# First LayerNorm shared between VectorE and ScalarE, with a new load order, five staging buffers and a split K load, in a fused attention and gated-GLU kernel

## Chip, cores and metric

The kernel runs on one core of one Trainium2 chip. The metric is device time in microseconds (us) for one launch. Eight runs of the kernel before took between 320.76 and 323.88 us, with a median of 322.65 us.

## What is computed

The input is 2048 rows (the sequence) by 640 features, in bf16. A LayerNorm without weights is followed by two branches that read the same normalized rows: causal attention with a sliding window of 256 keys in 32 heads of 20 features, and a gated unit with 1536 hidden features. The output is the sum of the input and both branches.

```python
xn = layernorm(A_x)                              # over 640 features, eps 1e-5
q, k, v = split(xn @ wqkv)                       # 32 heads of 20
p = softmax(mask(q @ k.T * 20 ** -0.5))          # 0 <= i - j < 256
attention = (p @ v) @ wo
h = sigmoid(xn @ w_gate) * (xn @ w_up)           # 2048 x 1536
out = A_x + attention + h @ w_down
```

## The kernel before

**Tiling.** The 2048 rows are handled as four chunks of 512 (`c`), each of four blocks of 128 rows (`s`). A chunk is normalized (`xn`, rows on the partitions) and transposed into `xnT` (features on the partitions). Chunk 0 is transposed by TensorE with an identity matrix and a copy out of PSUM (`transpose_block`, L266); chunks 1 to 3 by a transposing DMA (`turn_block`, L273).

**Projections.** `proj_block` (L283) makes 128 features of q or k for a whole chunk: five matmuls of 128x512 into one PSUM tile, a copy to a bf16 staging tile `st` (VectorE for q, ScalarE for k), and a DMA that stores it to a DRAM scratch (`sq`, `sk`). `spread` (L300) loads the scratch back as `qT` or `kT`, with each head at its own partitions. Ten such projections make a chunk: five for q, then five for k. Staging tiles rotate through the pool `stp` of four buffers; the first of them is first used as the zero operand of the warm-up matmuls. V is projected per block in two halves of 320 columns (`proj_v`, L313) and copied to `v`.

**Order of the work.** Every engine runs its instructions in the order in which the program issues them; there is no scheduler. The program has these stages.

- Start: loads are issued, mostly on SyncE's queue (SP): the four blocks of chunk 0 (two of them on ScalarE's queue), the V columns of `wqkv` in two pieces, its q and k columns, the first halves of the gate and up weights, chunk 1, and two DMAs (`clear`, L186) that write zeros into the scratch. Eleven matmuls on zeros keep TensorE busy in the meantime.
- First LayerNorm (L564 to L583): two blocks at a time. VectorE takes the statistics of a block in two halves and aggregates them (L243, L248), ScalarE takes the square root (L554), VectorE the reciprocal and the normalization (L558, L262), TensorE transposes, and ScalarE copies to `xnT` (L271). V projections are put between the steps of blocks 2 and 3, with copies on ScalarE.
- q and k of chunk 0 (`g_qk(0)`, L585), back to back.
- The main loop (L629). Each step issues the score matmuls, exponentials and masks of some heads, and then pulls as much other TensorE work from a list, `fill`, as a running credit allows. The list (L597 to L615) is in a fixed order: gate and up of chunk 0, q, k and V of chunk 1, two gate and up blocks of chunk 1, output of chunk 0, q and k of chunk 2, and so on. The LayerNorm of a later chunk is a generator (`g_norms`, L326) that `mix` (L543) draws from: one draw after every so many pieces of the host generator. For chunk 2 the hosts are `gu1a` (every second piece) and `out0` (every third piece).
- The end: the last output products with all of PSUM.

**Around the change in the main loop.** The `kT` load of chunks 1 to 3 is issued inside `g_v` (L362), after V of the first block; the four DMAs that rearrange the output weights `wo` in DRAM (`turn_wo`, L212) and the four that load them (`load_wo`, L217) stand behind it on SP's queue. The output rows `y` are staged in the pool `yp` of two buffers for chunks 0 to 2, and in the `xn` tiles (four buffers) for chunk 3.

PSUM tiles: one in `ps_a` (tile `acc`), three that rotate for all projections, gate, up and output (`ps_d`), and one of four times that size for scores.

Of the kernel before, what the change touches and what calls it, by code (L numbers as in the profile page):

```python
# [9 lines left out]
P = 128  # L10
S = 2048
D = 640
H = 32
DH = 20
F = 1536
DC = D // P
FC = F // P
CW = 512
NCH = S // CW
SBC = CW // P  # L20
HG = 4
NG = H // HG
GH = NG // 2
VW = DH + 1
# [5 lines left out]
ADD = mybir.AluOpType.add  # L30
MULT = mybir.AluOpType.mult
# [3 lines left out]
BF16 = mybir.dt.bfloat16  # L35
FP32 = mybir.dt.float32
EXP = mybir.ActivationFunctionType.Exp
TANH = mybir.ActivationFunctionType.Tanh
SQRT = mybir.ActivationFunctionType.Sqrt

U = 64
PTW = 10 * U
# [67 lines left out]
def kernel(  # L110
# [11 lines left out]
    nc = tc.nc  # L122
# [4 lines left out]
    def pool(name, bufs, **kw):  # L127
        return ctx.enter_context(tc.tile_pool(name=name, bufs=bufs, **kw))
# [2 lines left out]
    xp = pool("xp", 3)  # L131
    lnp = pool("lnp", 4)
    xtp = pool("xtp", 2)
    stp = pool("stp", 4)
    qp = pool("qp", 2)
    kp = pool("kp", 3)
    vp = pool("vp", 10)
# [3 lines left out]
    onp = pool("onp", 2)  # L141
    tp = pool("tp", 1)
    np_ = pool("np", 1)
    yp = pool("yp", 2)
    ps_a = pool("ps_a", 1, space=bass.MemoryType.PSUM)
    ps_d = pool("ps_d", 3, space=bass.MemoryType.PSUM)
    banks = ctx.enter_context(ExitStack())
# [5 lines left out]
    xc = {}  # L153
# [15 lines left out]
    def load_wqkv(part):  # L169
        nc.sync.dma_start(out=wqkv[:, :, part * D:(part + 1) * D],  # L170
                          in_=wqkv_r[:, :, part * D:(part + 1) * D])

    xc[0] = xp.tile([P, SBC, D], BF16, name="xc")
    for s, queue in ((0, nc.sync), (1, nc.scalar), (2, nc.sync), (3, nc.scalar)):
        queue.dma_start(out=xc[0][:, s, :], in_=xr[:, s, :])
    for d in (slice(0, 3), slice(3, DC)):
        nc.sync.dma_start(out=wqkv[:, d, 2 * D:], in_=wqkv_r[:, d, 2 * D:])
    load_wqkv(0)
    load_wqkv(1)

# [46 lines left out]
    eps = const.tile([P, 1], FP32, name="eps")  # L227
    nc.gpsimd.memset(eps, EPS)
    scr = const.tile([P, 1], FP32, name="scr")
    nc.scalar.activation(out=scr, in_=eps, func=SQRT)  # L230
    for n in (6, 5):
        ps = ps_d.tile([P, CW], FP32, name="pwarm", tag="d")
        for k in range(n):
            nc.tensor.matmul(ps, lhsT=warm[:, 0:P], rhs=warm, start=(k == 0), stop=(k == n - 1))


    xnT = {}
    xns = {}

    def ln_half(c, s, a, stats=None):  # L240
        if a == 0:
            stats = lnp.tile([P, 2, nc.vector.BN_STATS_DIM], FP32, name="stats")
        nc.vector.bn_stats(out=stats[:, a, :], in_=xc[c][:, s, a * HALF:(a + 1) * HALF])  # L243
        return stats

    def ln_mv(stats):
        mv = lnp.tile([P, nc.vector.BN_AGGR_DIM], FP32, name="mv")
        nc.vector.bn_aggr(out=mv, in_=stats)  # L248
        return mv

    def ln_block(c, s):
        return ln_mv(ln_half(c, s, 1, ln_half(c, s, 0)))
# [5 lines left out]
        return rstd  # L258

    def norm_block(c, s, mv, rstd):  # L260
        xn = lnp.tile([P, D], BF16, name="xn", bufs=4)
        nc.vector.tensor_scalar(out=xn, in0=xc[c][:, s, :], scalar1=mv[:, 0:1],  # L262
                                scalar2=rstd[:, 0:1], op0=SUB, op1=MULT)
        xns[c, s] = xn

    def transpose_block(c, s):  # L266
        xn = xns.pop((c, s))
        pt = ps_d.tile([P, DC, P], BF16, name="pt", tag="d")
        for d in range(DC):
            nc.tensor.transpose(pt[:, d, :], xn[:, d * P:(d + 1) * P], ident)  # L270
        nc.scalar.copy(out=xnT[c][:, :, s * P:(s + 1) * P], in_=pt)  # L271

    def turn_block(c, s):  # L273
        nc.sync.dma_start(out=xnT[c][:, :, s * P:(s + 1) * P], in_=xns.pop((c, s)), transpose=True)
# [1 line left out]
    def new_xnT(c):  # L276
        xnT[c] = xtp.tile([P, DC, CW], BF16, name="xnT")
# [3 lines left out]
    vt = {}  # L281
# [18 lines left out]
    def spread(w, c, g0, g1):  # L300

        if g0 == 0:
            qk[w, c] = (qp if w == "q" else kp).tile([P, NG, CW], BF16, name=w + "T")
        src = scratch[w, c % 2].rearrange("(g p) s -> p g s", p=P)
        nc.sync.dma_start(out=qk[w, c][:, g0:g1, :], in_=src[:, g0:g1, :])

    def new_v(c, s):
        v = vp.tile([P, H * VW + 11], BF16, name="v")
        vt[c * SBC + s] = v
        nc.gpsimd.memset(v[:, 0:H * VW].rearrange("p (h d) -> p h d", d=VW)[:, :, DH:VW], 0.5)  # L310
        nc.gpsimd.memset(v[:, H * VW:], 0.0)

    def proj_v(c, s, hf):  # L313
        v3 = vt[c * SBC + s][:, 0:H * VW].rearrange("p (h d) -> p h d", d=VW)
        ps = ps_d.tile([P, CW], FP32, name="pv", tag="d")
        for d in range(DC):
            nc.tensor.matmul(ps[:, 0:HALF], lhsT=xnT[c][:, d, s * P:(s + 1) * P],  # L317
                             rhs=wqkv[:, d, 2 * D + hf * HALF:2 * D + (hf + 1) * HALF],
                             start=(d == 0), stop=(d == DC - 1))
        copy = nc.vector.tensor_copy if c else nc.scalar.copy  # L320
        copy(out=v3[:, hf * 16:(hf + 1) * 16, 0:DH],  # L321
             in_=ps[:, 0:HALF].rearrange("p (h d) -> p h d", d=DH))

    MM = 216

# [36 lines left out]
    def g_v(c):  # L362
        for s in range(SBC):
            new_v(c, s)
            for hf in range(2):
                proj_v(c, s, hf)
            if s == 0:
                spread("k", c, 0, NG)
            yield 10 * 136


# [36 lines left out]

    def outp(c, s, ys, last=False):
        sb = c * SBC + s  # L410
        if c == NCH - 1:
            y = lnp.tile([P, D], BF16, name="xn", bufs=4)
        else:
            y = yp.tile([P, D], BF16, name="y_sb")

        def wo_half(hf):
            for m in range(DC):
                nc.tensor.matmul(ys[hf], lhsT=oc[c, m][:, s * P:(s + 1) * P],  # L418
                                 rhs=wo[:, m, hf * HALF:(hf + 1) * HALF],
                                 start=False, stop=(m == DC - 1))  # L420

        def add_half(hf):
            nc.vector.scalar_tensor_tensor(  # L423
                out=y[:, hf * HALF:(hf + 1) * HALF], in0=ys[hf], scalar=0.5,
                in1=xc[c][:, s, hf * HALF:(hf + 1) * HALF], op0=MULT, op1=ADD)

        if last:
            for hf in range(2):
                wo_half(hf)
                add_half(hf)  # L430
                cut = slice(hf * HALF, (hf + 1) * HALF)
                (nc.scalar, nc.sync)[hf].dma_start(out=out2[sb * P:(sb + 1) * P, cut], in_=y[:, cut])
        else:
            wo_half(0)
            wo_half(1)
            add_half(0)
            add_half(1)
            nc.sync.dma_start(out=out2[sb * P:(sb + 1) * P, :], in_=y)
        yield 10 * 136

    def g_out(c):
        for s in range(SBC):
            ys = [ps_d.tile([P, CW], FP32, name=f"y{i}", tag="d")[:, 0:HALF] for i in range(2)]
            yield from down(c, s, ys)
            yield from outp(c, s, ys)
# [97 lines left out]
    def mix(a, b, first, every=1, rest=True):  # L543

        for k, cost in enumerate(a):
            yield cost
            if k >= first and (k - first) % every == 0:
                yield next(b, 0)
        if rest:
            yield from b  # L550

    def root(mv):
        r = lnp.tile([P, 1], FP32, name="rstd")
        nc.scalar.activation(out=r, in_=mv[:, 1:2], func=SQRT, bias=eps)  # L554
        return r

    def norm_turn(s, mv, r):
        nc.vector.reciprocal(r, r)  # L558
        norm_block(0, s, mv, r)

    new_xnT(0)
    for s in range(SBC):
        new_v(0, s)
    for s in (0, 2):  # L564
        mv0 = ln_block(0, s)
        r0 = root(mv0)
        if s:
            proj_v(0, 0, 0)
            proj_v(0, 0, 1)
        half = ln_half(0, s + 1, 0)  # L570
        norm_turn(s, mv0, r0)
        mv1 = ln_mv(ln_half(0, s + 1, 1, half))
        r1 = root(mv1)
        if s:
            proj_v(0, 1, 0)
        transpose_block(0, s)
        norm_turn(s + 1, mv1, r1)
        if s:
            proj_v(0, 1, 1)
        transpose_block(0, s + 1)  # L580
    for s in (2, 3):
        for hf in range(2):
            proj_v(0, s, hf)  # L583
    nc.scalar.activation(out=scr, in_=neghalf, func=EXP)
    for _ in g_qk(0):  # L585
        pass
# [2 lines left out]
    fill = Fill()  # L589
    GU = 10 * MM  # L590
    OUT = 4 * 34 * 136
    def later(load, *args):
        load(*args)
        yield 0

    norms2 = g_norms(2, True)
# [5 lines left out]
    fill.add("wo_i", later(turn_wo), 0)  # L602
    fill.add("gu1a", mix(g_gu(1, 0, 2), norms2, 0, 2, False), 2 * GU)
    fill.add("wo", later(load_wo), 0)
    fill.add("out0", mix(g_out(0), norms2, 0, 3), OUT)
    fill.add("x3", later(load_x, 3), 0)
    fill.add("qk2", g_qk(2), 50 * MM)
    fill.add("v2", g_v(2), 40 * 136)
# [37 lines left out]
    c = NCH - 1  # L646
# [15 lines left out]
    for s in range(SBC):  # L662
        run(outp(c, s, ys[s], s == SBC - 1))
# [28 lines left out]
```

## Time and profile before

The profiled execution took 326.08 us, of which the span from the first to the last instruction is 324.0 us; its mean granted TensorE clock is 0.995.

| engine | busy us | share of the span | instructions |
|---|---|---|---|
| TensorE matmuls (PE) | 310.6 | 96% | 4391 |
| TensorE weight loads (PEld) | 174.6 | 54% | 4391 |
| ScalarE (ACT) | 192.4 | 59% | 240 |
| GpSimd (POOL) | 177.6 | 55% | 417 |
| VectorE (DVE) | 159.6 | 49% | 325 |

Some rows of the first 16 us, from the groups by line and shape:

| line, engine | what | count | mean ns |
|---|---|---|---|
| L243 DVE | statistics of half a block, 128x320 | 8 | 473 |
| L248 DVE | aggregate | 4 | 209 |
| L554 ACT | square root, 128x1 | 4 | 295 |
| L558 DVE | reciprocal, 128x1 | 4 | 164 |
| L262 DVE | normalize, 128x640 bf16 | 4 | 446 |
| L271 ACT | copy of a transposed block out of PSUM, 128x640 bf16 | 4 | 687 |
| L321 ACT | copy of half a V block out of PSUM, 128x320 | 8 | 426 |

Times are from the start of the span. In a list in order of time, each row has its start, its length, the engine, the line, the operation, what it writes and reads, the shape and a count; in brackets is how long the engine was idle before, and what ended that wait. SPq is SyncE's queue of DMA issues: its times are those of issuing a DMA, not of its transfer. Transfers land later. PEclk is the granted TensorE clock as a share of the full one.

### The profile page before, as it was taken

The numbers are of one execution on the slowest core, as the hardware profiler recorded it, in microseconds if no ns is written. First come the engines' busy times: TensorE is split into PE (matmuls) and PEld (weight loads), VectorE is DVE, ScalarE is ACT, GpSimd is POOL, SyncE is SP. The second block draws the span as 40 slices with busy tenths as digits, with TensorE's granted clock in tenths as the row PEclk, the third lists the DMA queues.
The fourth block names the chain that finished last, engine by engine and source line by source line (L and its number), as shares of the span: only waits on it lengthen the run. The fifth ranks groups of instructions, "written<-read, shape, count | busy, mean of one in ns | idle before, by whom it ended". The sixth has DMA issues, their size and how long they took to land.

```text
span 324.0 us, 10258 instructions
## 1 busy us (share of the span) xinstructions
PE 310.6 (96%) x4391; PEld 174.6 (54%) x4391; DVE 159.6 (49%) x325; ACT 192.4 (59%) x240; POOL 177.6 (55%) x417
## 2 busy tenths in 40 slices
PE   6979999999899979999999999999999999999996
PEld 2634444455466645644466655544456664444674
DVE  5330287574864433745954352754352444463224
ACT  3803586878564447766665457566766568778200
POOL 3000269567586827475793647556474857586400
PEclk9997999999999999999999999999999999999999
DMA  7964786946641452540035123710000000000002
GB/s 247 375 250 129 262 297 76 292 151 197 206 128 42 92 146 85 181 131 3 2 22 89 36 71 91 243 45 3 2 2 22 23 26 21 2 2 2 0 2 81
DMA packets 34380, 33.05 MB, mean 102 GB/s; under 512 B 9600, under 2 KB 33792, under 8 KB 34304
## 3 DMA queue, kind: packets, MB, share of 16 engines
q1 hardware_dynamic: 33904, 32.01, 33.2%
q8 instruction: 34, 0.56, 0.7%
q10 hardware_dynamic: 432, 0.41, 0.4%
q14 instruction: 10, 0.08, 0.1%
HBM read 21.00 MB, written 10.26 MB: 96 GB/s over the span
## 4 chain that ended last, share of the span: by engine, by line
PE 78%; DMA 9%; DVE 6%; ACT 2%; POOL 2%; issue 1%; SPq 1%; DVEq 0%; ACTq 0%; POOLq 0%
PE pg L382 14%; PE pu L389 13%; PE y L402 13%; PE pqk L290 12%; PE ps L455 7%; PE acc L486 6%; PE y L418 6%; PE pv L317 4%; DMA sq<-st 2%; DMA wo_i<-in_A_wo_dram 2%; PE d L402 2%; DMA sk<-st 1%; DMA xnT<-xn 1%; POOL pT L465 1%; ACT pT L461 1%
## 5 line engine op out<-in xcount | busy, mean ns | idle before, releaser
L465 POOL TENSOR_SCALAR_AFFINE_SELECT pT<-pT 128x256 bf16<-128x256 bf16 (+1 forms) x352 | 163.0, 497 | 124.5 <-ACT pT L461 124.4
L461 ACT ACTIVATE pT<-ps 128x1280 bf16<-128x1280 f32 (+2 forms) x152 | 147.4, 1023 | 72.6 <-PE ps L455 64.5
L393 DVE SCALAR_TENSOR_TENSOR h<-th,pu 128x512 bf16<-128x512 f32 x48 | 32.8, 684 | 59.2 <-PE pu L389 34.6
L382 PE MATMUL pg<-xnT,wg 128*128 128x512 bf16 x240 | 59.8, 380 | 0.3 <-DVE h L393 0.3
L389 PE MATMUL pu<-xnT,wu 128*128 128x512 bf16 x240 | 59.8, 380 | 0.0
L290 PE MATMUL pqk<-xnT,wqkv 128*128 128x512 bf16 x200 | 47.9, 391 | 4.2 <-DVE st L294 2.5
L402 PE MATMUL y<-wd,h 128*128 128x320 bf16 x336 | 49.4, 300 | 0.0
L402 PEld LDWEIGHTS <-h 128*128 128x128 bf16 x384 | 36.1, 98 | 14.4 <-issue 0.2
L496 DVE STREAM_TRANSPOSE t<-acc 128x512 f32<-128x512 f32 x32 | 22.8, 712 | 33.6 <-PE acc L486 33.3
L385 ACT ACTIVATE th<-pg 128x512 f32<-128x512 f32 x48 | 28.9, 603 | 17.3 <-DVE h L393 9.7
L389 PEld LDWEIGHTS <-wu 128*128 128x128 bf16 x240 | 22.0, 98 | 25.4 <-issue 0.6
L382 PEld LDWEIGHTS <-wg 128*128 128x128 bf16 x240 | 22.0, 98 | 25.2 <-issue 0.8
L290 PEld LDWEIGHTS <-wqkv 128*128 128x128 bf16 x200 | 22.6, 120 | 24.0 <-issue 7.6
L455 PE MATMUL ps<-qT,kT 20*64 20x64 bf16 (+3 forms) x2048 | 32.8, 232 | 1.9 <-DMA kT<-sk 1.3
L455 PEld LDWEIGHTS <-kT 20*64 20x64 bf16 x2048 | 22.2, 104 | 21.6 <-issue 16.4
L486 PE MATMUL acc<-pT,v 128*32 128x128 bf16 (+2 forms) x928 | 25.7, 250 | 0.0
L486 PEld LDWEIGHTS <-v 128*32 128x32 bf16 x928 | 16.9, 97 | 15.3 <-issue 11.4
L317 PE MATMUL pv<-wqkv,xnT 128*128 128x320 bf16 x160 | 24.0, 299 | 0.5 <-DVE v L321 0.4
L423 DVE SCALAR_TENSOR_TENSOR y_sb<-y,xc 128x320 bf16<-128x320 f32 x24 | 11.6, 490 | 24.0 <-PE y L418 24.0
L294 DVE CAST st<-pqk 128x512 bf16<-128x512 f32 x20 | 13.7, 691 | 18.6 <-PE pqk L290 14.3
L418 PE MATMUL y<-wo,oc 128*128 128x320 bf16 x140 | 21.2, 299 | 0.3 <-DMA wo<-wo_i 0.3
L502 DVE TENSOR_TENSOR on<-t,rec 128x320 bf16<-128x320 f32 (+4 forms) x48 | 20.3, 422 | 1.1
(42 smaller groups left out, 152.4 us busy)
## 6 DMA issues: line engine op xcount, KB each, us to landing
qT<-sq SPq DMA_DIRECT2D x3, 1024.0 KB, 5.7
kT<-sk SPq DMA_DIRECT2D x3, 1024.0 KB, 5.5
sq<-st SPq DMA_DIRECT2D x20, 128.0 KB, 2.2
sk<-st SPq DMA_DIRECT2D x20, 128.0 KB, 3.1
wg<-in_B_w_gate_dram SPq DMA_DIRECT2D x2, 960.0 KB, 11.7
wu<-in_B_w_up_dram SPq DMA_DIRECT2D x2, 960.0 KB
xc<-in_A_x_dram SPq DMA_DIRECT2D x3, 640.0 KB, 11.8
wd<-in_B_w_down_dram SPq DMA_DIRECT2D x1, 1920.0 KB
```

Source lines behind the costliest of these rows:

```text
L290: nc.tensor.matmul(ps, lhsT=wt[:, m, :], rhs=xnT[c][:, d, :], start=(d == 0), stop=(d == DC - 1))
L317: nc.tensor.matmul(ps[:, 0:HALF], lhsT=xnT[c][:, d, s * P:(s + 1) * P], rhs=wqkv[:, d, 2 * D + hf * HALF:2 * D + (hf + 1) * HALF], start=( ...
L382: nc.tensor.matmul(pg, lhsT=part(wg, d, f), rhs=xnT[c][:, d, :], start=(d == 0), stop=(d == DC - 1))
L385: nc.scalar.activation(out=th, in_=pg, func=TANH, scale=0.5)
L389: nc.tensor.matmul(pu, lhsT=part(wu, d, f), rhs=xnT[c][:, d, :], start=(d == 0), stop=(d == DC - 1))
L393: nc.vector.scalar_tensor_tensor(out=h, in0=th, scalar=1.0, in1=pu, op0=ADD, op1=MULT)
L402: nc.tensor.matmul(ys[hf], lhsT=ht[c, f][:, s * P:(s + 1) * P], rhs=wd[:, f, hf * HALF:(hf + 1) * HALF], start=(f == 0), stop=False)
L418: nc.tensor.matmul(ys[hf], lhsT=oc[c, m][:, s * P:(s + 1) * P], rhs=wo[:, m, hf * HALF:(hf + 1) * HALF], start=False, stop=(m == DC - 1))
L455: nc.tensor.matmul(ps[hf * U:(hf + 1) * U, i, col * U:(col + n) * U], lhsT=qk["k", kc][32 * i:32 * i + DH, g, key:key + U], rhs=qk["q", c] ...
L461: nc.scalar.activation(out=pt[:, :, to * U:(to + n) * U], in_=ps[:, :, col * U:(col + n) * U], func=EXP, scale=SCALE)
L465: nc.gpsimd.affine_select(out=out, in_=in_, pattern=[[0, HG], [sign, pattern]], compare_op=GE, fill=0.0, base=base, channel_multiplier=-sign)
L486: nc.tensor.matmul(acc[32 * i:32 * i + 32, q * U:(q + n) * U], lhsT=v[:, h * VW:h * VW + 32], rhs=pt[:, i, col * U:(col + n) * U], start=( ...
```

## The change

Five edits are made at once.

- **First LayerNorm.** For blocks 1 and 3, ScalarE takes the statistics: one pass with Identity and a scale of -1/640 that accumulates the negated mean, one with Square and that mean as bias that accumulates the squared deviations, and a root. VectorE keeps blocks 0 and 2, the reciprocals and all normalizations. Copies out of PSUM are shared between ScalarE and VectorE, and the transposes of blocks 0, 2 and 3 use the tile of `ps_a`. V projections are placed anew between these steps.
- **Load order.** V's columns of `wqkv` are issued ahead of blocks 2 and 3, and block 3 goes from ScalarE's queue to SP's. Thirteen warm-up matmuls in place of eleven.
- **Buffers.** `stp` has five staging buffers in place of four. The pool `yp` is gone: all output rows use the `xn` tiles, of which there are five.
- **K load.** `kT` of chunks 1 to 3 is loaded in two DMAs: head groups 0 and 1, then the other six.
- **Normalization of chunk 2.** `out0` draws from it after every second piece in place of every third.

```diff
-    stp = pool("stp", 4)
+    stp = pool("stp", 5)
...
-    yp = pool("yp", 2)
...
-    for s, queue in ((0, nc.sync), (1, nc.scalar), (2, nc.sync), (3, nc.scalar)):
+
+    def load_rows(s, queue):
         queue.dma_start(out=xc[0][:, s, :], in_=xr[:, s, :])
+
+    load_rows(0, nc.sync)
+    load_rows(1, nc.scalar)
     for d in (slice(0, 3), slice(3, DC)):
         nc.sync.dma_start(out=wqkv[:, d, 2 * D:], in_=wqkv_r[:, d, 2 * D:])
+    load_rows(2, nc.sync)
+    load_rows(3, nc.sync)
     load_wqkv(0)
     load_wqkv(1)
...
-    for n in (6, 5):
+    for n in (7, 6):
...
-        xn = lnp.tile([P, D], BF16, name="xn", bufs=4)
+        xn = lnp.tile([P, D], BF16, name="xn", bufs=5)
...
-    def transpose_block(c, s):
+    def transpose_block(c, s, home=ps_d, tag="d", copy=nc.scalar.copy):
         xn = xns.pop((c, s))
-        pt = ps_d.tile([P, DC, P], BF16, name="pt", tag="d")
+        pt = home.tile([P, DC, P], BF16, name="pt", tag=tag)
         for d in range(DC):
             nc.tensor.transpose(pt[:, d, :], xn[:, d * P:(d + 1) * P], ident)
-        nc.scalar.copy(out=xnT[c][:, :, s * P:(s + 1) * P], in_=pt)
+        copy(out=xnT[c][:, :, s * P:(s + 1) * P], in_=pt)
...
             if s == 0:
-                spread("k", c, 0, NG)
+                spread("k", c, 0, 2)
+                spread("k", c, 2, NG)
...
-        if c == NCH - 1:
-            y = lnp.tile([P, D], BF16, name="xn", bufs=4)
-        else:
-            y = yp.tile([P, D], BF16, name="y_sb")
+        y = lnp.tile([P, D], BF16, name="xn", bufs=5)
...
+    def mean_act(s):
+        xn = lnp.tile([P, D], BF16, name="xn", bufs=5)
+        neg = lnp.tile([P, 1], FP32, name="neg")
+        nc.scalar.activation(out=xn, in_=xc[0][:, s, :], func=IDENTITY, scale=-1.0 / D, accum_out=neg)
+        return xn, neg
+
+    def root_act(s, xn, neg):
+        r = lnp.tile([P, 1], FP32, name="rstd")
+        nc.scalar.activation(out=xn, in_=xc[0][:, s, :], func=SQUARE, bias=neg, accum_out=r)
+        nc.scalar.activation(out=r, in_=r, func=SQRT, bias=eps, scale=1.0 / D)
+        return r
+
+    def norm_act(s, xn, neg, r):
+        nc.vector.reciprocal(r, r)
+        nc.vector.tensor_scalar(out=xn, in0=xc[0][:, s, :], scalar1=neg[:, 0:1],
+                                scalar2=r[:, 0:1], op0=ADD, op1=MULT)
+        xns[0, s] = xn
...
+    act, dve = nc.scalar.copy, nc.vector.tensor_copy
+    mv0 = ln_block(0, 0)
+    xn1, neg1 = mean_act(1)
+    r1 = root_act(1, xn1, neg1)
+    r0 = root(mv0)
+    norm(0, mv0, r0)
+    norm_act(1, xn1, neg1, r1)
+    transpose_block(0, 0, ps_a, "acc", dve)
+    xn3, neg3 = mean_act(3)
+    transpose_block(0, 1, ps_d, "d", act)
+    mv2 = ln_block(0, 2)
+    r2 = root(mv2)
+    proj_v(0, 0, 0, act)
+    r3 = root_act(3, xn3, neg3)
+    norm(2, mv2, r2)
+    proj_v(0, 0, 1, dve)
+    v10 = project_v(0, 1, 0)
+    transpose_block(0, 2, ps_a, "acc", dve)
+    norm_act(3, xn3, neg3, r3)
+    copy_v(0, 1, 0, v10, dve)
+    proj_v(0, 1, 1, act)
+    proj_v(0, 2, 0, act)
+    transpose_block(0, 3, ps_a, "acc", dve)
+    proj_v(0, 2, 1, act)
+    proj_v(0, 3, 0, act)
+    proj_v(0, 3, 1, act)
...
-    fill.add("out0", mix(g_out(0), norms2, 0, 3), OUT)
+    fill.add("out0", mix(g_out(0), norms2, 0, 2), OUT)
```

`project_v` and `copy_v` are the two halves of the former `proj_v`; `norm` is the former `norm_turn`. The order of the score, output and gate matmuls on TensorE is the same in both kernels; TensorE's order differs in the first stage alone.

## The prediction

> **What bounds the kernel now.** I read the page's first part, then TensorE's waits one by one, then the lists in order of time around the longest of them. TensorE's matmuls are busy for 96% of the span, and the chain of waits is 78% TensorE.
>
> ```profile
> PE 310.6 (96%) x4391; PEld 174.6 (54%) x4391; DVE 159.6 (49%) x325; ACT 192.4 (59%) x240; POOL 177.6 (55%) x417
> ...
> PE 78%; DMA 9%; DVE 6%; ACT 2%; POOL 2%; issue 1%; SPq 1%; DVEq 0%; ACTq 0%; POOLq 0%
> ```
>
> The change removes no matmul of the answer (it adds two of the warm-up). So it can gain only where TensorE stands still or runs slowly. Its waits by releaser:
>
> ```profile
> PE pqk L290 <- DVE st L294: 2.5, 1, 2.5
> PE pqk L290 <- DMA xnT<-xn: 1.7, 1, 1.7
> PE pt L270 <- DVE xn L262: 1.7, 2, 1.2
> PE ps L455 <- DMA kT<-sk: 1.3, 1, 1.3
> ...
> PE y L418 <- DMA wo<-wo_i: 0.3, 1, 0.3
> ```
>
> Four of these five are addressed: `st` by the fifth buffer, `xnT` by the earlier draws, `kT` by the split load, `xn` by the LayerNorm. I take them in order of time. The first has a second cost, which the windows show (columns: window, length, busy time and count of PE, PEld, DVE, ACT, POOL, PEclk, DMA share, GB/s):
>
> ```profile
> 14.30:22.00 7.70, 7.70 (x37) 4.13 (x36) 2.77 (x4) 1.91 (x3) 0.00 (x0) 1.00 0.97 347
> 22.00:24.60 2.60, 0.11 (x2) 0.05 (x1) 0.69 (x1) 0.51 (x2) 0.00 (x0) 1.00 0.06 24
> 24.60:29.60 5.00, 5.00 (x16) 2.03 (x16) 0.00 (x0) 1.74 (x4) 0.00 (x0) 0.66 0.53 157
> ```
>
> Until 22 us the DMA engines are full (0.97); then TensorE stops, and afterwards it runs at 0.66 of its clock.
>
> **Fifth staging buffer.**
>
> ```profile
> 23.80 0.69 DVE L294 CAST st<-pqk 128x512 bf16<-128x512 f32 x1 [4.25 <-DMA sq<-st]
> 24.09 1.07 ACT L296 CAST st<-pqk 128x512 bf16<-128x512 f32 x2 [7.61 <-DMA sq<-st]
> 24.55 5.08 PE L290 MATMUL pqk<-xnT,wqkv 128*128 128x512 bf16 x15 [2.49 <-DVE st L294]
> ```
>
> The warm-up took staging buffer 1, so the fifth q copy takes the buffer of the first and waits until its store has landed, at 23.8 us, behind everything queued since the start. Three PSUM tiles let TensorE finish two k projections beyond that copy; it stops at 22.06, and the last three projections run from 24.55 to 29.63. With five buffers the fifth q copy is free, and the first k copy is the one that waits for 23.8. TensorE gets one projection further (eight of ten). The first k copy ends at 23.80 + 0.59 (L296) = 24.4; two projections remain, at 1.08 us each (the 35 matmuls in 7.72 us before the stall, with the last one's tail): **end at 26.6 in place of 29.63, 3.0 us less**. Of that 1.35 us is the stall proper and 1.7 us the clock: 5.08 us for three projections instead of 3.4.
>
> Here a rule and the trace differ. The Trainium skill, "TensorE: Matmul & The Clock Gate", section "Why this matters for your kernels", asks only that gaps between matmuls stay under some 3 us; by it a stall of 2.49 us costs no clock, and the gain would be 1.35. The row says the clock did fall after 2.49 us. The same section's page calls the window free-running, so it may fall in some runs and not in others. I take the row for the profiled execution and half of it (0.85 us) for the median; 0 and 1.7 are kept as ends. The new stall is some 0.8 us (next part), which I take to leave the clock alone, as the waits of 1.34 and 1.72 us did (mean clock 0.995).
>
> The time of landing is what I cannot know. The bytes ahead of the store are the same, and the DMA engines are 97% busy until 22 us, so I leave it at 23.8, with 0.7 us either way.
>
> **First LayerNorm and load order.** The chain that ends in q's start, from the row durations of before (hand-over 0.05 us):
>
> - Block 1 has landed by 3.9 us. ScalarE: mean 3.92 to 4.61, squares to 5.35, root to 5.69. The root of block 0, ready at 4.85, is queued behind these, to 5.94 (before: 5.18).
> - VectorE: block 0 normalized by 6.63 (before 5.87), block 1 by 7.24 (before 7.52).
> - VectorE's copy of block 0: 640 elements by the slope of L294 (512 in 0.69, of which some 0.16 is fixed) is 0.82, to 8.03. Statistics of block 2 to 9.17, its root to 9.50, normalized by 10.19; V copy; copy of block 2 to 11.56; block 3 normalized by 12.16 (before 11.28).
> - Transposes at 12.29, copy 12.78 to 13.61, the two V halves of block 3 to 15.0. **q starts at 15.0, not at 14.34.**
>
> So VectorE loses two blocks of statistics (2 x 1.16 us) but gets three copies of 0.82 and two of 0.49 (L321 on VectorE later): it is not relieved. The passes with accumulation have no row; 0.69 each (L271's size) is the low end, and 0.98 (one more small ACTIVATE each) the high one, with q at 15.5. The other unknown is VectorE's copy. "VectorE: DVE Perf Modes", section "Why PSUM operands drop a tier", allows bf16 from PSUM the double rate, which makes it 0.5 and q's start 14.2. The only PSUM copies in the trace are fp32, at the single rate; I take 0.82 and keep 14.2 to 15.5.
>
> None of these moves the end. From q's start S, the ninth projection is due at S + 8.65: 23.65 for S = 15.0, against 24.4 for the freed buffer. Up to S = 15.75 the store's landing decides. This edit, the load order (V's columns, 0.8 MB, pass 0.33 MB of rows; block 3 would land some 2.5 us later, near 7.3, before ScalarE needs it) and the two warm-up matmuls (before the first transpose, by 6.2 us) cost and gain nothing; without that cover each us of delay costs one. The work after q and k (six gate and up halves of 1.08, then scores at 36.04 before, `kT` landed by 34.5) moves with it.
>
> **Split K load.**
>
> ```profile
> 81.98 0.39 SPq L305 DMA_DIRECT2D kT<-sk  x1
> 82.42 2.80 SPq L214 DMA_DIRECT2D wo_i<-in_A_wo_dram  x4
> 88.44 3.53 SPq L219 DMA_DIRECT2D wo<-wo_i  x4
> ...
> 87.52 0.43 PE L455 MATMUL ps<-qT,kT 20*64 20x320 bf16 x28 [1.34 <-DMA kT<-sk]
> ...
> 95.33 1.52 PE L418 MATMUL y<-wo,oc 128*128 128x320 bf16 x10 [0.31 <-DMA wo<-wo_i]
> ```
>
> 1 MB is issued at 81.98 and awaited until 87.5. The first 256 KB should land in 3.4 us (the row of `qT` loads of that size), at 85.4, before TensorE asks at 86.18. So 1.34 us go. But what is late next stands in the same list: `wo` travels behind `kT` on the same queue, lands at about 95.2 whatever TensorE does, and TensorE already waits 0.31 us for it. It will now arrive at 93.7 and wait 1.65. **Net 0**, at worst -0.4 if the one more issue (0.4 us on SP) reaches the landing; I expect it hidden, since `wo`'s issues wait for transfers, not for SP. For chunks 2 and 3 TensorE shows no wait for `kT`: nothing.
>
> **Draws of chunk 2's LayerNorm.**
>
> ```profile
> 104.16 1.26 SPq L274 DMA_TRANSPOSE xnT<-xn  x1
> ...
> 109.22 3.85 SPq L274 DMA_TRANSPOSE xnT<-xn  x3
> ...
> 116.32 1.25 PE L290 MATMUL pqk<-xnT,wqkv 128*128 128x512 bf16 x5 [1.72 <-DMA xnT<-xn]
> ```
>
> q of chunk 2 is due at 114.6, but the last of four transposes is issued at 111.85 and lands at 116.1. `g_norms` needs nine draws, two in `gu1a` and seven in `out0`: at pieces 0, 3, ... 18 of its 20 before, at 0, 2, ... 12 after. On SP's queue the last three transposes move ahead of the third output store, behind the second (103.76): issued at 104.2, 105.4 and 106.6, landed by 111 with the 4.2 us of the slowest. That is over 3 us early: **1.72 us less**. The draws' VectorE work (normalizations of 0.44 us) lies beside TensorE; POOL's last `rstd` (106.3 to 107.2 before) moves up by a step too.
>
> **One ring of five rows for `xn` and `y`.** Each write waits for the DMA of the tile five allocations earlier. The closest pair is the third output row of `out0` (107.6) after the first normalized block, transposed by about 102 and landed by 106: it doesn't wait. Cost 0.
>
> **Sum.** Against the profiled execution: 3.0 + 0 + 0 + 1.72 = 4.75 us, 326.08 to 321.3, span 324.0 to 319.3. That execution is 3.4 us above the median of 322.65, and its clock row explains half of that at most. For the median: 1.35 + 0.85 + 1.72 = 3.9, so **318.8 us**. The likeliest case's own range is 317.2 to 320.2 (clock 0.85 and landing 0.7 either way).
>
> **Rivals.** A difference under 0.5% (1.6 us) can't be told from none here.
>
> - *The LayerNorm takes over as the bound* (12%). ScalarE's passes, or block 3 late in the queue with ScalarE's copy of block 1 behind its mean, bring q to 17.0; the last k then ends at 17.0 + 10.8 = 27.8 in place of 26.6. Against it: 1.2 us are needed beyond the cover, and the high end has none. Time 320.0.
> - *Only one of the two gains arrives* (15%): POOL's `rstd` holds VectorE, so `xnT` is late again, or the store lands at 25.5 because some DMA engines run behind. For it: 2.6 us between full engines and landing are unexplained. Time 322.65 - 2.2 = 320.5.
> - *It does nothing that counts* (12%): with the clock unaffected in most runs, the 1.35 us come back as a wait for the first `kT`, and the 1.72 as a longer wait for `wo`. Time 322.3.
> - *The shared ring makes it slower* (6%). VectorE works in order: a `y` addition that waits for a transpose holds h and q copies behind it, and three PSUM tiles cover about one projection (1.08 us). Eight output rows follow transposes in `out0` and `out1`; if each waits 2 us, TensorE loses 0.9 each, 7.2, and the time is 322.65 - 3.9 + 7.2 = 326. It decides once a transpose lands after the addition five tiles later; by the trace some 2 us are missing for that.
>
> The forecast has 55%. Faster by over 0.5%: the forecast and nearly all of the first two, 0.80. Within: the third and a remainder, 0.13. Slower: 0.07. The range for 8 in 10 is 316.8 to 321.3: below, clock and landing both full; above, the second rival with some drift between runs.
>
> **What would show it.** Right: the tenth projection ends near 26.6 with the clock at 1.0 and the first k copy ends a wait for `sq`; no wait for `kT` at about 83; a wait for `wo` of some 1.7 us; none for `xnT`. Wrong: q starting after 15.75, the clock at half after the new stall, or TensorE waiting for `h` or `st` while a `y` addition waits for a DMA.

## The result and the profile after

The changed kernel takes 319.54 us (median of 19 runs) against 322.97 us before (54 runs): ratio 0.9911, 95% interval 0.9891 to 0.9930. The medians are 3.4 us apart; the ratio, which is not that of the medians, gives 2.9 us (2.3 to 3.5). The forecast was 3.9 us.

One of the 30 executions of the changed kernel that were recorded, the one profiled first, took 619.77 us with TensorE at half speed throughout, and is left aside until the last section; the profile here is of another execution of the same kernel (`after_again`), which took 319.78 us with a span of 317.8 us.

TensorE's waits of the kernel after, in the view that was shown for before:

```profile
PE y L428 <- DMA wo<-wo_i: 1.2, 1, 1.2
...
PE pt L277 <- DVE xn L269: 0.5, 1, 0.5
PE pqk L297 <- ACT st L303: 0.4, 1, 0.4
```

The four waits that the change addressed are gone or short: 2.5 us for `st` became 0.4, the waits for `xnT` and `kT` are no longer listed, and 1.7 us for the first LayerNorm became 0.5. One grew: `wo`, from 0.3 to 1.2 us. The windows around the first stall (the same columns as before; the edges follow this execution's events):

```profile
14.20:22.00 7.80, 7.75 (x37) 4.28 (x37) 3.45 (x5) 1.93 (x4) 0.00 (x0) 1.00 1.00 357
22.00:23.43 1.43, 1.07 (x5) 0.47 (x4) 0.00 (x0) 0.64 (x2) 0.00 (x0) 1.00 0.23 77
23.43:25.80 2.37, 2.37 (x11) 1.25 (x11) 0.00 (x0) 1.52 (x4) 0.00 (x0) 1.00 0.34 112
```

TensorE is busy for 1.07 of the 1.43 us in which it had stood still for most of the time, and the clock behind it is 1.00 instead of 0.66. The DMA engines are as full as before until 22 us. In order of time:

```profile
22.79 1.56 ACT L303 CAST st<-pqk 128x512 bf16<-128x512 f32 x3 [6.38 <-DMA sq<-st]
...
23.43 2.32 PE L297 MATMUL pqk<-xnT,wqkv 128*128 128x512 bf16 x10 [0.36 <-ACT st L303]
```

It is now ScalarE's first k copy that waits for a store, and only two projections (ten matmuls) are left behind it. They end at 25.75 us; before, the last one ended at 29.63. Farther on:

```profile
77.87 0.90 SPq L312 DMA_DIRECT2D kT<-sk  x2
...
90.93 1.52 PE L428 MATMUL y<-wo,oc 128*128 128x320 bf16 x10 [1.20 <-DMA wo<-wo_i]
```

Both loads of `kT` are issued at 77.87, the score matmuls of chunk 1 start without a wait, and TensorE stands before the first product with `wo`.

Where the 6.2 us between the two profiled spans went, by the lead of the changed kernel at the same instruction: 3.9 us at the end of the projections of chunk 0 (2.1 of stall, 1.7 of clock), 5.3 us at the arrival at `wo` (1.3 more, the wait for `kT`), 4.4 us behind it (0.9 given back), 6.3 us at q of chunk 2 (1.72 of it the wait for `xnT`), 6.2 us at the end. The profiled execution of before took 3.1 us more than its median, so this is more than the medians' 3.4.

### The profile page after: what moved, and what is told of

It is laid out like the page before. It is cut to its first block, busy times and chain, and to the rows that moved or that the text cites. A ratio compares the mean times of both kernels' runs of the same rounds, so it can differ in the third digit from the quotient of the medians.

```text
span 617.8 us, 10276 instructions
## 1 busy us (share of the span) xinstructions
PE 613.3 (99%) x4393; PEld 254.8 (41%) x4393; DVE 161.9 (26%) x324; ACT 198.2 (32%) x243; POOL 177.9 (29%) x417
## 4 chain that ended last, share of the span: by engine, by line
PE 99%; DVE 0%; issue 0%
PE pg L395 18%; PE pu L402 18%; PE y L415 16%; PE pqk L297 15%; PE pv L323 8%; PE acc L496 7%; PE y L428 7%; PE ps L465 6%; PE d L415 2%; PE pwarm L241 1%; PE d L428 1%; PE acc L415 1%; PE pt L277 0%; PE acc L428 0%; DVE xnT L278 0%; DVE xn L433 0%
## 5 line engine op out<-in xcount | busy, mean ns | idle before, releaser
L395 PE MATMUL pg<-xnT,wg 128*128 128x512 bf16 x240 | 119.9, 670 | 0.0
L402 PE MATMUL pu<-xnT,wu 128*128 128x512 bf16 x240 | 119.7, 671 | 0.0
L415 PE MATMUL y<-wd,h 128*128 128x320 bf16 x336 | 100.2, 497 | 0.0
L297 PE MATMUL pqk<-xnT,wqkv 128*128 128x512 bf16 x200 | 95.2, 672 | 0.0
L415 PEld LDWEIGHTS <-h 128*128 128x128 bf16 x384 | 54.0, 144 | 50.1 <-issue 15.6
L323 PE MATMUL pv<-wqkv,xnT 128*128 128x320 bf16 x160 | 48.0, 500 | 0.1
L496 PE MATMUL acc<-pT,v 128*32 128x128 bf16 (+2 forms) x928 | 44.5, 370 | 0.0
L428 PE MATMUL y<-wo,oc 128*128 128x320 bf16 x140 | 43.0, 503 | 0.0
L433 DVE SCALAR_TENSOR_TENSOR xn<-y,xc 128x320 bf16<-128x320 f32 x28 | 13.8, 492 | 93.9 <-PE y L428 93.8
L428 PEld LDWEIGHTS <-oc 128*128 128x128 bf16 x160 | 23.5, 149 | 21.5 <-issue 6.9
L323 PEld LDWEIGHTS <-xnT 128*128 128x128 bf16 x160 | 22.6, 145 | 21.6 <-issue 7.8
```

The source lines that it names most:

```text
L297: nc.tensor.matmul(ps, lhsT=wt[:, m, :], rhs=xnT[c][:, d, :], start=(d == 0), stop=(d == DC - 1))
L395: nc.tensor.matmul(pg, lhsT=part(wg, d, f), rhs=xnT[c][:, d, :], start=(d == 0), stop=(d == DC - 1))
L402: nc.tensor.matmul(pu, lhsT=part(wu, d, f), rhs=xnT[c][:, d, :], start=(d == 0), stop=(d == DC - 1))
L415: nc.tensor.matmul(ys[hf], lhsT=ht[c, f][:, s * P:(s + 1) * P], rhs=wd[:, f, hf * HALF:(hf + 1) * HALF], start=(f == 0), stop=False)
L496: nc.tensor.matmul(acc[32 * i:32 * i + 32, q * U:(q + n) * U], lhsT=v[:, h * VW:h * VW + 32], rhs=pt[:, i, col * U:(col + n) * U], start=( ...
```

## The experiments

Ratios are against the kernel before in the same series of runs, since the three series ran on three chips (`after_again` and b1 to b3; a1 to a4; a5 to a8): the kernel before had medians of 321.89, 322.92 and 322.99 us in them. The changed kernel itself ran only in the first, so the a runs are set against it through the kernel before.

| run | what it is | median us | ratio (95% interval) |
|---|---|---|---|
| after_again | the changed kernel | 319.52 | 0.9922 (0.9889 to 0.9955) |
| b1_stp5_ring | before + fifth buffer and shared ring | 321.42 | 0.9978 (0.9954 to 1.0003) |
| b2_draws | before + earlier draws | 320.96 | 0.9960 (0.9938 to 0.9982) |
| b3_ksplit | before + split K load | 323.13 | 1.0034 (1.0014 to 1.0055) |
| a1_stp4 | changed, four buffers | 321.10 | 0.9965 (0.9945 to 0.9986) |
| a2_draws3 | changed, draws as before | 321.44 | 0.9966 (0.9945 to 0.9987) |
| a3_k1load | changed, one K load | 319.84 | 0.9916 (0.9885 to 0.9948) |
| a4_oldln | changed, LayerNorm and loads as before | 320.48 | 0.9937 (0.9916 to 0.9957) |
| a6_oldload | changed, load order as before | 320.34 | 0.9935 (0.9913 to 0.9958) |
| a7_oldstats | changed, LayerNorm steps as before | 320.53 | 0.9933 (0.9906 to 0.9959) |
| a5_wo_early | changed, `wo` moved early | 319.70 | 0.9903 (0.9879 to 0.9927) |
| a8_wo_early_k1 | the same with one K load | 320.43 | 0.9939 (0.9917 to 0.9961) |

**The changed kernel again.**

> The changed kernel once more, for a profile at the full TensorE clock. Theory (gain from two TensorE waits and the clock after the first): median near 319.5 us, tenth projection of chunk 0 ends near 26.6 us with the clock at 1.0, no wait for kT near 83 us, a wait for wo of about 1.65 us, none for xnT of chunk 2. Rival (the LayerNorm stage carries the gain): q of chunk 0 starts well before 14.3 us.

The theory's marks are met but for two sizes: the tenth projection ends at 25.75, not 26.6, and the wait for `wo` is 1.20, not 1.65. By its own mark the rival is out: q starts at 14.27 us against 14.34 before.

**One edit alone, on the kernel before.**

```diff
-    stp = pool("stp", 4)
+    stp = pool("stp", 5)
-    yp = pool("yp", 2)
...
-        xn = lnp.tile([P, D], BF16, name="xn", bufs=4)
+        xn = lnp.tile([P, D], BF16, name="xn", bufs=5)
```

> The kernel before with five staging buffers and the shared ring of five xn/y rows alone (the fifth buffer does not fit beside the pool yp). Theory: TensorE gets one projection further before it waits for the first store (stall about 1.4 us in place of 2.5), the clock stays up; 1.1 us less than before, 2.8 us less against executions of before with the clock dip, so a median near 320.7 us. Rival (the LayerNorm stage carries the gain): within 0.5 us of before.

Only 0.7 us less, with an interval that includes no change: by its time this run doesn't part the theory from its rival. The stall itself is gone in its trace:

```profile
15.48 10.96 PE L289 MATMUL pqk<-xnT,wqkv 128*128 128x512 bf16 x49
26.27 1.24 PE L381 MATMUL pg<-xnT,wg 128*128 128x512 bf16 x4
```

All ten projections run in one piece. But they start at 15.48 instead of 14.34, which itself covers part of the wait for the store (the first k copy starts at 23.30), and the clock fell in two other places (windows, as above):

```profile
7.40:10.84 3.44, 3.27 (x16) 2.13 (x17) 2.69 (x9) 1.33 (x4) 0.00 (x0) 0.50 1.05 380
...
112.70:117.00 4.30, 4.25 (x38) 1.75 (x40) 0.69 (x1) 1.87 (x2) 0.41 (x1) 0.60 0.58 183
```

The first is behind the waits of the first LayerNorm (0.77 and 1.20 us with 0.46 us of matmuls between), the second behind the wait for `xnT`, which in this execution is 1.99 us. So a stall that goes at one place doesn't keep the clock up at the others.

```diff
-    fill.add("out0", mix(g_out(0), norms2, 0, 3), OUT)
+    fill.add("out0", mix(g_out(0), norms2, 0, 2), OUT)
```

> The kernel before with the draws of chunk 2's LayerNorm after every second piece alone. Theory: the wait of 1.72 us for xnT of chunk 2 goes and nothing takes its place: 1.7 us less, median near 321.2 us. Rival (the time comes back as a wait on POOL's rstd or in the next projections): within 0.5 us of before.

1.3 us less in the ratio (0.6 to 2.0), of 1.7 forecast. In the trace the wait for `xnT` is gone and none stands in its place. The rival is out.

```diff
-                spread("k", c, 0, NG)
+                spread("k", c, 0, 2)
+                spread("k", c, 2, NG)
```

> The kernel before with kT of chunks 1 to 3 in two loads alone. Theory: the wait of 1.34 us for kT goes and comes back as a longer wait for wo (0.31 to about 1.65 us): median unchanged within 0.5 us. Rival (wo lands earlier, or the wait for wo is covered): 1.3 us less.

No gain, as the theory said, but 1.1 us slower, which it did not. TensorE's order in this run:

```profile
83.82 0.43 PE L456 MATMUL ps<-qT,kT 20*64 20x320 bf16 x28
...
93.21 1.52 PE L419 MATMUL y<-wo,oc 128*128 128x320 bf16 x10 [1.89 <-DMA wo<-wo_i]
```

The scores at 83.82 have no wait in front of them; `wo` has one of 1.89 us, where before had 1.34 and 0.31 at the two places. That accounts for 0.24 us. The other 0.9 us are in neither of these waits; the times show that more executions fall into the slower of two groups, which the kernel before has too (last section).

**One edit undone, on the changed kernel.**

```diff
-    stp = pool("stp", 5)
+    stp = pool("stp", 4)
```

> The changed kernel with four staging buffers. Theory (waits removed, and with them the clock dips that a wait of about 1.7 us or more brings in a part of the executions): TensorE stops two projections earlier, a stall of some 1.4 to 2.5 us; 1.1 us slower without a dip (fastest near 320.0 us), 1.7 more with one, so a median of 320.2 to 321.7 us and a wider spread. Rival (dips come by chance, whatever the waits): 1.1 us slower, 320.6 us, with the narrow spread of the changed kernel.

1.6 us slower than the changed kernel (0.9965 against 0.9911 and 0.9922, mean 0.9916, of 323). TensorE's waits:

```profile
PE pqk L297 <- DVE st L301: 1.5, 1, 1.5
```

The stall is back with 1.48 us and without a fall of the clock behind it. The size is that of the theory, the narrow spread (21 of 22 runs between 320.45 and 322.1) is that of the rival: a dip came in one run of 22.

```diff
-    fill.add("out0", mix(g_out(0), norms2, 0, 2), OUT)
+    fill.add("out0", mix(g_out(0), norms2, 0, 3), OUT)
```

> The changed kernel with the draws of chunk 2's LayerNorm after every third piece again. Theory: the wait for xnT of chunk 2 is back at 1.7 to 2.0 us; fastest near 320.6 us, 1.7 us more in the executions with a dip behind that wait, median 321 to 322.3 us. Rival (dips by chance): median 321.2 us with a narrow spread. Rival (the draws gave nothing in this company): 319.5 us.

1.6 us slower; the wait for `xnT` is back with 1.67 us:

```profile
PE pqk L297 <- DMA xnT<-xn: 1.7, 1, 1.7
```

This edit is worth its wait in both companies. Here too dips were rarer than the theory had them (1 of 22).

```diff
-                spread("k", c, 0, 2)
-                spread("k", c, 2, NG)
+                spread("k", c, 0, NG)
```

> The changed kernel with kT of chunks 1 to 3 in one load again. Theory (the split's gain is given back at wo): a wait of about 1.3 us for kT is back, and the wait for wo falls from 1.20 to some 0.3 us; within 0.5 us of the changed kernel, 319.1 to 320.0 us. Rival (the split gains by itself): 1.2 us slower, 320.7 us.

Equal to the changed kernel, over six runs. TensorE's waits show the exchange:

```profile
PE ps L464 <- DMA kT<-sk: 1.1, 1, 1.1
```

There is no line for `wo` any more: 1.05 us before the scores in place of 1.20 before `wo`. The split's gain is given back 7.5 us later (scores at 82.23, wait from 89.73 in the changed kernel).

```diff
     load_rows(0, nc.sync)
     load_rows(1, nc.scalar)
+    load_rows(2, nc.sync)
+    load_rows(3, nc.scalar)
...
-    load_rows(2, nc.sync)
-    load_rows(3, nc.sync)
...
-    for n in (7, 6):
+    for n in (6, 5):
...
+    for s in (0, 2):
+        mv0 = ln_block(0, s)
+        r0 = root(mv0)
...
```

> The changed kernel with the first LayerNorm, its load order and its eleven warm-up matmuls as before. Theory (the landing of the first q store sets the end of the projections of chunk 0): q starts within 0.3 us of 14.27 us, or up to 1.2 us later when the clock dips in this stage (TensorE idles 1.2 and some 0.6 us there); both are covered; within 0.5 us of the changed kernel, 319.1 to 320.0 us. Rival (the LayerNorm carries gain): 1 us or more slower, 320.5 us.

0.7 us slower than the changed kernel, between theory and rival, with intervals that overlap. In its profile q starts at 14.23 us, as in the changed kernel, and the first k copy at 23.15 instead of 22.79. The next two runs split the stage to see whether that is the load order. First the load order alone:

```diff
     load_rows(0, nc.sync)
     load_rows(1, nc.scalar)
+    load_rows(2, nc.sync)
+    load_rows(3, nc.scalar)
...
-    load_rows(2, nc.sync)
-    load_rows(3, nc.sync)
```

> The changed kernel with the old load order alone (blocks 2 and 3 ahead of V's columns, block 3 on ScalarE's queue). Theory (the load order makes the first q store land some 0.7 us earlier, and that is the 1 us which undoing the whole stage cost): the first k copy starts near 23.2 us in place of 22.4, median 320.2 to 320.5 us. Rival (the shared statistics make it): 319.5 us.

Then the steps and the warm-up alone:

```diff
-    for n in (7, 6):
+    for n in (6, 5):
...
+    for s in (0, 2):
+        mv0 = ln_block(0, s)
+        r0 = root(mv0)
...
```

> The changed kernel with the old LayerNorm steps and warm-up, but the new load order. Theory (the load order makes the difference): the first k copy starts near 22.4 us, median 319.5 us. Rival (the shared statistics make it): 320.2 to 320.5 us.

By the ratio both are some 0.6 us slower, with intervals that reach the changed kernel's; neither half shows as the cause alone. The profiles give no place for it: the first k copy starts at 22.45 with the old load order and 22.16 with the old steps, both earlier than in the profile of the changed kernel, and gate and up start at 25.24 and 25.09 (25.59 there). The theory that the load order brings the store earlier falls with that. What the first stage is worth, and where, stays open between 0 and about 1 us.

**The wait for `wo` taken away.** Its eight DMAs depend on nothing that the kernel computes, so they can stand earlier on SP's queue.

```diff
     load_rest()
+    turn_wo()
...
+    fill.add("wo", later(load_wo), 0)
     fill.add("x2", later(load_x, 2), 0)
...
-    fill.add("wo_i", later(turn_wo), 0)
...
-    fill.add("wo", later(load_wo), 0)
```

> The changed kernel with the rearranging of wo issued right after the last loads of chunk 0's stage, and wo's load ahead of chunk 2's rows, some 40 us before its use. Theory (the split's gain was given back at wo): the wait of 1.20 us for wo goes and nothing takes its place, 318.3 us. Rival (the moved transfers delay the q stores of chunk 1 or another load by as much): 319.5 us.

No gain that can be told (0.9903 against 0.9911 and 0.9922). The wait for `wo` is gone, and a new one is 20 us ahead of it:

```profile
67.29 0.58 ACT L303 CAST st<-pqk 128x512 bf16<-128x512 f32 x1 [1.93 <-DVE rec L508]
67.77 1.95 ACT L471 ACTIVATE pT<-ps 128x1280 bf16<-128x1280 f32 x2
...
69.77 0.42 PE L465 MATMUL ps<-qT,kT 20*64 20x320 bf16 x16 [0.94 <-ACT pT L471]
```

The view names VectorE for ScalarE's idle 1.93 us, but `rec` had long been made. The copy takes the staging buffer of the first q store of chunk 1, and in the trace that store lands at 67.14 us, behind `wd` (66.77), whose issue the four loads of `wo` have pushed back from 53.40 to 54.67. In the changed kernel the same copy runs at 66.25. Behind it in ScalarE's order stand the exponentials, and TensorE waits 0.94 us for them. So the rival was right: what the moved transfers saved at `wo` they cost at another transfer on the queue.

The same with `kT` in one load:

```diff
-                spread("k", c, 0, 2)
-                spread("k", c, 2, NG)
+                spread("k", c, 0, NG)
```

> As the run with wo early, but kT of chunks 1 to 3 in one load. Theory: a wait of 1.05 to 1.34 us for kT is back and has no longer wait for wo to hide in, so about 1.2 us slower than with the split: 319.5 us. Rival (the split is worth nothing of its own): 318.3 us.

A wait of 0.71 us for `kT` is back, `wo` waits no more, and the ratio is 0.36% higher (1.2 us), with intervals that overlap. This fits the theory that the split is worth something only where `wo` is not the next to be late, but does not show it.

## Why the prediction was right, point by point

**Fifth buffer: right, larger.** Forecast was an end of the projections at 26.6; it was 25.75. TensorE got one projection further, as worked out. The term that was off is the landing of the first store: first k copy at 22.79 instead of 23.80. The first copy that waits for that store started between 22.0 and 23.3 us in the twelve other profiles, so 23.80 was a late one, and the 0.7 us kept either way was too little. Undone, the edit costs 1.6 us.

**The clock: right for the execution, too large for the median.** After the new stall of 0.36 us the clock stays at 1.00. But the half of 1.7 us put into the median was too much. Of 174 executions of before whose clock is recorded, 68 have a mean clock of 0.995 or less, what one dip of 3.41 us at half speed makes of 320 us. Their median is 323.0 us, and that of the other 106 is 322.2: 0.8 us apart (0.7, 1.3 and 0.0 on the three chips). So a dip in 39% of the executions is worth some 0.3 us of the median by this estimate, not 0.85. One reason that a dip can cost less than 1.7 us stands in b2_draws: it had one from 7.6 to 11.0 us, in the first LayerNorm, its q started at 15.47, and the wait for the store, 0.61 instead of 2.49 us, took most of that in. Against the 106 without a dip the changed kernel (319.5) is 2.7 us faster, and 1.9 us on the chip of `after_again` alone, where the waits alone were forecast at 1.35 + 1.72 = 3.1.

The term was also put down to the wrong edit. With the fifth buffer alone (b1) 7 of 22 executions still have a dip, and with the stall back (a1) one of 22. The dips are linked more closely to the first LayerNorm, to which the prediction gave no part in the clock: with its old steps in the changed kernel (a4, a7) 6 of 33 have one, with the new ones 5 of 132 (last section).

Here the Trainium skill's rule in "TensorE: Matmul & The Clock Gate", section "Why this matters for your kernels" (no gap over some 3 us), was weighed against a row with a dip behind 2.49 us, and the row was taken. The runs bear the row out and go lower: dips stand behind waits of 1.79 (b3_ksplit), 1.98 (a4_oldln) and 1.99 us (b1_stp5_ring), and in b1 and b2 behind two waits, 0.77 or 0.56 and then 1.20 us. But 1.89 us in b3 brought none, nor did 1.72 us in before. What parts them is where the idle time lies. A dip lasts 3.41 us, and within a trace the clock changes only whole multiples of 3.41 us apart (in b1 at 7.43 and 113.24, 31 steps). These are such steps, counted from the changes of each trace (columns as before): two of b2, two of before, three of b3.

```profile
4.18:7.59 3.41, 1.65 (x13) 0.73 (x12) 2.91 (x10) 1.17 (x3) 0.00 (x0) 1.00 0.92 274
7.59:11.00 3.41, 3.41 (x17) 2.00 (x16) 2.37 (x8) 1.49 (x4) 0.00 (x0) 0.50 1.05 381
...
113.79:117.20 3.41, 1.69 (x11) 0.87 (x9) 0.98 (x2) 1.47 (x2) 0.21 (x1) 1.00 0.36 73
117.20:120.61 3.41, 3.41 (x43) 1.88 (x42) 1.74 (x3) 1.94 (x2) 0.86 (x3) 1.00 0.63 215
...
88.60:92.01 3.41, 2.72 (x49) 1.58 (x47) 3.20 (x8) 2.48 (x4) 3.33 (x9) 1.00 0.70 205
92.01:95.42 3.41, 2.21 (x16) 1.49 (x16) 1.15 (x3) 0.50 (x1) 2.05 (x5) 1.00 0.01 1
95.42:98.83 3.41, 3.41 (x63) 2.34 (x66) 0.19 (x1) 1.94 (x2) 1.13 (x3) 1.00 0.16 53
```

In b2 TensorE is busy for 1.65 of 3.41 us, so idle for 1.76, and the next step runs at half the clock. In before it is idle for 1.72, and the clock stays. In b3 an edge splits the wait of 1.89 us into 0.69 and 1.20. In the thirteen profiles with a clock record, behind the warm-up, a dip follows each of the six steps with 1.76 us or more of idle time (up to 2.49) and none of those with 1.72 or less. The step in which the matmuls end is left out: there 1.85 us brought no fall in `after_again`. So it is the idle time within one step that decides here, at about half a step, and not the length of one gap.

**First LayerNorm: right that it doesn't set the end of the stage, wrong in its parts.** q was put at 15.0 and started at 14.27. The groups by line and shape of the kernel after:

```profile
L580 ACT ACTIVATE xn<-xc,neg 128x640 bf16<-128x640 bf16 x2 | 1.7, 830 | 0.0
L575 ACT ACTIVATE xn<-xc 128x640 bf16<-128x640 bf16 x2 | 1.5, 736 | 2.5 <-DMA xc<-in_A_x_dram 2.5
L278 DVE COPY xnT<-pt 128x640 bf16<-128x640 bf16 x3 | 1.5, 491 | 0.4 <-PE pt L277 0.3
...
L580 ACT ACTIVATION_READ_ACCUMULATOR xn<-xc,neg 128x1 f32 x2 | 0.4, 190 | 0.0
```

VectorE's copy out of PSUM takes 0.49 us for 640 bf16 elements, not the 0.82 that the slope of the fp32 copies gave. The rule in "VectorE: DVE Perf Modes", section "Why PSUM operands drop a tier", allows a bf16 source in PSUM the double rate; the estimate from it was 0.5, and it was right against my choice of the row; the row nearest in operation was of the wrong type. ScalarE's passes take 0.74 and 0.83 us, and each brings a second instruction of 0.19 us that reads the accumulator: 0.92 and 1.02, at and above the high end of the 0.69 to 0.98 that were kept. The errors oppose each other, and q's start shows that the first weighs more. What was not seen is the stage's part in the clock, which the last section counts, and up to some 0.7 us in the median whose place stays open.

**Split K load: right.** The wait went and came back at `wo`; 1.20 instead of 1.65 us, because `wo` landed 13.1 us behind the last k store instead of 13.8. Undoing it changes nothing. That it cost 1.1 us alone was not foreseen.

**Draws: right.** The last three transposes are issued from 100.14 us on, and q of chunk 2 starts at 110.04 behind the last output product without a wait:

```profile
100.14 4.85 SPq L281 DMA_TRANSPOSE xnT<-xn  x3
...
110.04 1.24 PE L297 MATMUL pqk<-xnT,wqkv 128*128 128x512 bf16 x4
```

Worth 1.3 us alone and 1.6 when undone, of 1.72.

**Shared ring: right.** No TensorE wait in the trace of the kernel after goes back to an output row. What the edit is for can be read from the sizes: `yp` held two rows of 1.25 KB per partition, and the room goes to one `xn` row (1.25 KB) and the fifth staging buffer (1 KB).

The sum was 3.9 us against 2.9 by the ratio and 3.4 by the medians, with some 0.5 too much for the clock and up to 0.7 too little for the first stage. That these two offset each other is luck; the two waits that carry the forecast are not. The edits don't add up: alone, three of them give -0.7, -1.3 and +1.1 us, and undone one by one, four of them cost 1.6, 1.6, 0.0 and 0.7 us, against 2.7 us for all together by the mean ratio.

## What to carry to other kernels

When an edit removes a wait of a transfer, read on along the same queue to the next transfer and to who needs it: here the gain of 1.3 us lasted 7.5 us, and moving that next transfer away pushed back a third. Where one buffer decides a stall, ask which instruction gets the freed buffer and what its landing time is; the gain is the work that can be done until then, not the stall. For a copy whose type or source isn't in the trace, a rate written down for that type can be nearer than a row of another type.

## What the hardware showed beside it

- **The first LayerNorm's waits and the clock.** Of the executions with VectorE's statistics as before (before, b1, b2, b3, a4, a7), 93 of 273 have a mean clock of 0.995 or less; with ScalarE's share (changed, a1, a2, a3, a5, a6, a8), 5 of 132, the 619.77 us execution not counted. In four of the six traces of the first group TensorE idles for 1.20 us and for another 0.4 to 0.8 us within 2 us of it; in the second group it idles for 0 to 1.13 us in the whole stage behind the warm-up. That fits the idle time within a step as the cause: the pairs of 1.97 us (b1) and 1.76 us (b2) brought a dip, those of 1.70 (before) and 1.61 us (a7) did not. But not every dip of the first group lies in this stage: in the profile of before it followed the stall at 22 us.
- **A clock that never rose.** The execution of 619.77 us has no change of the clock recorded (its PEclk reads 1.00), and its matmuls of 128x512 keep TensorE busy for twice the time from first to last (groups by line):

```profile
L395 PE MATMUL pg<-xnT,wg 128*128 128x512 bf16 x240 | 119.9, 670 | 0.0
L402 PE MATMUL pu<-xnT,wu 128*128 128x512 bf16 x240 | 119.7, 671 | 0.0
```

  Before, the same two groups took 59.8 us each, with a mean of 380 ns. TensorE was busy for 613.3 of 617.8 us, so it was not for want of work. It was seen once, and its cause is open.
- **Two groups of times before.** Without a recorded dip, the kernel before has many executions near 321.2 and many near 323.2 us. On the chip of the b runs 15 of 34 took more than 322 us. With the earlier draws alone (b2) none of 17 did; with the split K load alone (b3) it was 13 of 15, though the fastest of b3 took hardly longer than the fastest before (320.95 against 320.78). So in the kernel before the slower group goes with the late draws, and most of what b3 lost is a greater share of executions in that group. The changed kernel lies within 318.9 to 320.3 us but for three of 29. What happens in the slower group is not shown: the one profile of that kernel is of an execution with a dip.
